# Attention into two dense blocks on one core: fifteen matmuls of the third output moved ahead, a third accumulator bank, and another tile for the convolution's products

## The chip, the core and the metric

The kernel runs on one core of one Trainium2 chip. A core has five instruction streams that run beside one another: TensorE does matmuls and transposes (PE in the profile, with its weight loads as PEld), VectorE is DVE, ScalarE is ACT, GpSimd is POOL, and SyncE (SP) issues the transfers of this kernel. Each engine takes its instructions in a fixed order, and one that waits holds up all behind it on the same engine. The metric is the time of the device in microseconds, the median over runs; less is better.

## The reference, cut to what matters

```python
# q, k, v: (4, 12, 448, 64); weights are 768 x 768, w_tok_*: 448 x 448, 64-bit floats
scores = q @ k.T / sqrt(64), masked above the diagonal
x      = softmax(scores) @ v                     # (4, 448, 768) after joining the heads
gate   = sigmoid(causal convolution of x, 5 taps for each channel)
x      = (gate * (x @ w_val)) @ w_out
theta  = x @ w_theta
y      = w_tok_r @ (x * cos(theta)) + w_tok_i @ (x * sin(theta))   # mixes the 448 positions
u      = x + y
out    = u + relu(u @ w_ch)
```

## The kernel before

The work of a batch falls in two: attention, in six pairs of heads (a pair fills 128 partitions, and makes 128 channels of x), and a dense part of four products with 768 x 768 weights and the token mixing. A product is made in six outputs of 128 channels, numbered n over the whole program: n = 0 to 5 are `w_val`, 6 to 11 `w_out`, and so on. An output takes 18 matmuls (`gemm`, L550): six pieces of the contraction, each with three matmuls, since x and the weights are each split in a high and a low part (`x_hi`, `x_lo`, `w_hl`). The weights come as 64-bit floats. `load_w` fetches half an output (`cv_raw`), `to_f32` makes 32-bit floats of it (DVE L178, ACT, DVE L182, with a bank of PSUM between), and `split_w` the two parts; from n = 3 on POOL does this (L117 high, L120 low).

Batch 0 has nothing to run beside its attention, so a prologue loop of 70 steps does attention of pairs 0 to 6, ten steps each, and the first weights. It also makes outputs 0 and 1 piece by piece, as each pair's x is ready (`gemm_ahead`, L529). After it `dense(b)` runs step by step, with the attention of the next batch woven in at a set rate. A pair's scores are made for pair g while pair g - 1 is transposed and multiplied by v (`attn_iter`). In batch 0 the convolution of pairs 0 to 5 runs on POOL (`attn_X2`, L495 to L502): a gate tile, a tile `tp` for a tap's product, and four adds. `hf` (L590) is gate times output.

Tiles come out of pools by tag: a tag has so many buffers, handed out in turn, and whoever gets a buffer waits until the one before is done with it. `tp` and `hf` share the tag "tmp" with two buffers. `tok_bits` (L191), the raw token weights, and z of the second block have the tag "z" with four. PSUM has eight banks: tag "mm" (accumulators) has two, tag "at" six, for attention's scores, transposes and products and for `to_f32`.

The framework's scheduler orders the instructions of each engine from the program's order, its own model of durations, and explicit constraints (`issue_after`). All transfers are on SP's one queue, which takes them in order. `plain` is a copy in device memory of the converted `w_val` and `w_out`, kept for the later batches.

Of the kernel before, what the change touches and what calls it, by code (L numbers as in the profile page):

```python
# [9 lines left out]
F32 = mybir.dt.float32  # L10
# [19 lines left out]
AHEAD = 2  # L30
# [12 lines left out]
PLAIN = (0, 1)  # L43
# [5 lines left out]
def kernel(  # L49
# [14 lines left out]
    nc = tc.nc  # L64
    B, H, S, D = q.shape
    DM = H * D
    P = 128
    CP = 112
    NC = S // CP
    NP = H // 2  # L70
    NQ = S // D
# [9 lines left out]
    KC = DM // P  # L81
# [3 lines left out]
    KH = KC // 2  # L85
    NW = 4 * KC
# [3 lines left out]
    pool = ctx.enter_context(tc.tile_pool(name="pool", bufs=2))  # L90
    ps = ctx.enter_context(tc.tile_pool(name="ps", bufs=2, space=PSUM))
# [5 lines left out]
    ident = cpool.tile([P, P], F32, name="ident")  # L97
# [13 lines left out]

    def psum(tag):
        at = "mm" if tag == "mm" else "at"
        return ps.tile([P, 512], F32, tag=at, name=f"ps_{tag}", bufs=2 if tag == "mm" else 6)

    def pool_hi(dst, src):
        nc.gpsimd.tensor_scalar(out=dst, in0=src, scalar1=1.0, scalar2=0.0, op0=ALU.mult, op1=ALU.add)  # L117
# [91 lines left out]
    scratch = dram.tile([NW, 2, P, 2 * KH * P], F32, name="scratch")  # L209
    plain = dram.tile([NW, 2, P, KH * P], F32, name="plain")  # L210
    bits = {}
    splits = {}

    def words(t):
        return t.rearrange("p n two -> p (n two)")[:, 0:CV]

    def load_w(n, g):
        if n >= NW:
            return
        e = n % KC  # L220
        t = pool.tile([P, CV, 2], I32, tag="wb", name="cv_raw", bufs=8)
        nc.sync.dma_start(
            out=t.rearrange("p (c n) two -> p c (n two)", c=KH),
            in_=stages[n // KC][g * KH * P : (g + 1) * KH * P, 2 * e * P : 2 * (e + 1) * P].rearrange(
                "(c p) n -> p c n", p=P
            ),
        )
        bits[n, g] = t

    def stage_w(n, g):  # L230
        if n < NW:
            to_f32(words(bits[n, g]), bits[n, g])

    def split_w(n, g):
        if (n, g) not in bits:
            return
        flat = words(bits.pop((n, g))).bitcast(F32)
        t = flat.rearrange("p (c n) -> p c n", n=P)
        kept = n % NW // KC in PLAIN
        if B > 1 and kept and n < NW:  # L240
            nc.sync.dma_start(out=plain[n, g], in_=flat)
        store = B > 1 and (kept and B > 2 if n >= NW else not kept)
        if n < AHEAD:
            hi, lo = (
                pool.tile([P, S], F32R, tag=tag, name="w_ahead", bufs=12)[:, : KH * P].rearrange("p (c n) -> p c n", n=P)
                for tag in ("act_hi", "act_lo")
            )
        else:
            hl = pool.tile([P, 2, KH, P], F32R, tag="wb", name="w_hl", bufs=8)
            hi, lo = hl[:, 0], hl[:, 1]  # L250
        if AHEAD < n < NW:
            pool_hi(hi, t)
        else:
            nc.scalar.copy(hi, t)  # L254
        (dve_lo if n <= AHEAD or n < NW and int(W_DVE[n // KC]) > g else pool_lo)(lo, t, hi)
        if store and n < AHEAD:
            for a, x in enumerate((hi, lo)):
                nc.sync.dma_start(
                    out=scratch[n, g][:, a * KH * P : (a + 1) * KH * P], in_=f32(x.rearrange("p c n -> p (c n)"))
                )  # L260
        elif store:
            nc.sync.dma_start(out=scratch[n % NW, g], in_=f32(hl.rearrange("p a c n -> p (a c n)")))
        splits[n, g] = (hi, lo)
# [22 lines left out]
    x_hl = {}  # L286
# [7 lines left out]
    av_ins = []  # L294
# [118 lines left out]
    def attn_R(g):  # L413
        if not 0 <= g < B * NP:
            return
        rec = pool.tile([P, NQ], F32, tag="rec", name="rec")
        nc.vector.tensor_scalar(out=rec, in0=sums[g], scalar1=1.0e-9, scalar2=None, op0=ALU.add)
        nc.vector.reciprocal(rec, rec)  # L418
        if g < NP:
            wide = pool.tile([P, NQ, D], F32, tag="m2k", name="wide", bufs=2)  # L420
            nc.vector.tensor_tensor(
                out=wide, in0=istack.unsqueeze(1).broadcast_to((P, NQ, D)),
                in1=rec.unsqueeze(2).broadcast_to((P, NQ, D)), op=ALU.mult,
            )
            wides[g] = wide
            return
        pt = psum("tr")
        nc.tensor.transpose(pt[:NQ, :P], rec, ident)
        rect = pool.tile([NQ, 2, D], F32, tag="rect", name="rect", bufs=1)
        nc.vector.tensor_copy(rect, pt[:NQ, :P].rearrange("i (j x) -> i j x", j=2))  # L430
        for j in range(2):
            nc.vector.tensor_copy(rect[0:3, j], pt[0:3, (1 - j) * D : (2 - j) * D])
        rows = dram.tile([2, NQ, D], F32, tag="rows", name="rows", bufs=2)
        nc.sync.dma_start(out=rows[:, 0:5].rearrange("h i x -> i h x"), in_=rect[2:NQ])
        nc.sync.dma_start(out=rows[:, 5:NQ].rearrange("h i x -> i h x"), in_=rect[0:2])
        row_at[g] = rows
# [46 lines left out]
    def attn_X2(g):  # L483
        b, hp = divmod(g, NP)
        x = xf[g % 2]
        gt = pool.tile([P, S], F32, tag="gate", name="gate", bufs=6)
        if CONV_ACT[g]:
            nc.scalar.activation(gt, x[:, 0:S], AF.Copy, scale=cw[:, 0, hp : hp + 1])
            for t in range(1, KW):
                tp = pool.tile([P, S], F32, tag="tmp", name="tp")  # L490
                nc.scalar.activation(tp, x[:, t : t + S], AF.Copy, scale=cw[:, t, hp : hp + 1])
                nc.gpsimd.tensor_tensor(out=gt, in0=gt, in1=tp, op=ALU.add)
        elif CONV_POOL[g]:
            tp = pool.tile([P, S], F32, tag="tmp", name="tp")
            nc.gpsimd.tensor_scalar(  # L495
                out=gt, in0=x[:, 0:S], scalar1=cw[:, 0, hp : hp + 1], scalar2=1.0, op0=ALU.mult, op1=ALU.mult
            )
            for t in range(1, KW):
                nc.gpsimd.tensor_scalar(  # L499
                    out=tp, in0=x[:, t : t + S], scalar1=cw[:, t, hp : hp + 1], scalar2=1.0, op0=ALU.mult, op1=ALU.mult  # L500
                )
                nc.gpsimd.tensor_tensor(out=gt, in0=gt, in1=tp, op=ALU.add)  # L502
        else:
            nc.vector.tensor_scalar(out=gt, in0=x[:, 0:S], scalar1=cw[:, 0, hp : hp + 1], scalar2=None, op0=ALU.mult)
            for t in range(1, KW):
                nc.vector.scalar_tensor_tensor(
                    out=gt, in0=x[:, t : t + S], scalar=cw[:, t, hp : hp + 1], in1=gt, op0=ALU.mult, op1=ALU.add
                )
        gates[b, hp] = gt
        raw_gates.append((b, hp))  # L510
# [6 lines left out]

    wn = [AHEAD]
    ahead = {}

    def gemm_ahead(kc):
        xhi, xlo = x_hl[0, kc]
# [11 lines left out]
                splits.pop((n, 0)), splits.pop((n, 1))  # L534


    def gemm(acts):
        n = wn[0]
        wn[0] += 1
        pt = psum("mm")  # L540
        for g in range(2):
            split_w(n + 1, g)
            stage_w(n + 2, g)
            load_w(n + 3, g)
            fetch_w(n + 3, g)
            whi, wlo = splits.pop((n, g))
            for kc in range(g * KH, (g + 1) * KH):
                xhi, xlo = acts[kc]
                for m, (a, x) in enumerate(((whi, xhi), (whi, xlo), (wlo, xhi))):
                    nc.tensor.matmul(  # L550
                        pt[:, :S], lhsT=a[:, kc % KH, :], rhs=x,
                        start=kc == 0 and m == 0, stop=kc == KC - 1 and m == 2,
                    )
            if g == 0:
                yield
        return pt
# [206 lines left out]
    for n in range(5 * H + 10):  # L763
        next(at, None)
        if n == 5:
            conv_raw = load_conv()
        if n == CONV_AT:
            setup_conv(conv_raw)
        if 1 <= n < 5 * H:
            with tc.issue_after(ttr_ins[-1].ins):  # L770
                for at_n, (m, g) in zip(A_TILES, ((0, 0), (1, 0), (0, 1), (1, 1), (2, 0), (2, 1), (3, 0), (3, 1))):
                    if n == max(W_FROM, at_n - W_AT):
                        load_w(m, g)
                    if n == at_n:
                        stage_w(m, g)
                        if m < AHEAD + 1:
                            split_w(m, g)
        if n >= 25 and n % 10 == 5:
            with tc.issue_after(av_ins[-1].ins):
                gemm_ahead(n // 10 - 2)  # L780
        if n == 5 * H + 9:
            gemm_ahead(KC - 1)
        if n == 5 * H - 3:
            with tc.issue_after(ttr_ins[-1].ins):
                for g in range(2):
                    load_w(AHEAD + 2, g)
# [47 lines left out]
```

## Time and profile before

| what | value |
|---|---|
| median of 3 runs | 699.96 us (698.92 to 702.09) |
| the profiled execution | 701.29 us, span 699.2 us, mean granted clock 0.989 |
| PE busy | 673.4 us, 96% of the span |
| DVE, ACT, POOL busy | 376.4, 358.8 and 302.2 us |

The span is from the first to the last instruction of the profiled execution; 2.09 us of its time lie around it. TensorE is busy nearly throughout, so what another engine does matters where TensorE waits for it. The granted clock is the share of full speed at which TensorE was let run.

### The profile page before, as it was taken

To read this page: it belongs to the slowest core of one execution; us is meant where nothing else is said; L and a number is where in the kernel's file an instruction comes from. 1 tells how busy PE (TensorE), PEld (TensorE's weight loads), DVE (VectorE), ACT (ScalarE), POOL (GpSimd) and SP (SyncE) were. 2 spreads that over 40 slices of the span, in tenths; PEclk is the share of its full clock that TensorE was granted. 3 is DMA by queue.
4 is the path that set the end of the run, shared out by engine and by line. 5 is a ranking of instruction groups with operands and counts; after the bars stand their busy time and mean duration, and the time that the engine had idled before them with its cause. 6 is when DMAs were issued, how large, how long until landed. Compare 5 with 4: busy or idle time off the path is not lost.

```text
span 699.2 us, 12863 instructions
## 1 busy us (share of the span) xinstructions
PE 673.4 (96%) x4595; PEld 582.9 (83%) x4595; DVE 376.4 (54%) x944; ACT 358.8 (51%) x849; POOL 302.2 (43%) x319
## 2 busy tenths in 40 slices
PE   5999799989999999999999999999999999999997
PEld 4777687868888898888898888888888999898996
DVE  4877696668565455345556444544765241126521
ACT  4787486759764545537654234337664221243401
POOL 0599958867485765742663000220601503011100
PEclk9999899999999999999999999999999999999999
DMA  8759478788442999897240776756230578772232
GB/s 212 169 158 228 123 220 267 211 296 249 130 150 71 297 302 301 274 297 193 82 119 13 222 212 213 214 175 184 84 105 14 159 213 222 209 220 69 86 105 66
DMA packets 133030, 124.67 MB, mean 178 GB/s; under 512 B 72905, under 2 KB 110567, under 8 KB 132967
## 3 DMA queue, kind: packets, MB, share of 16 engines
q1 hardware_dynamic: 132967, 123.86, 60.6%
q8 instruction: 36, 0.59, 0.4%
q14 instruction: 27, 0.22, 0.1%
HBM read 94.66 MB, written 29.16 MB: 177 GB/s over the span
## 4 chain that ended last, share of the span: by engine, by line
PE 79%; POOL 7%; DVE 5%; DMA 3%; ACT 3%; issue 2%; SPq 1%; DVEq 0%; POOLq 0%; ACTq 0%
PE ps_mm L550 44%; PE ps_mm L656 15%; PE ps_s L355 5%; PE ps_av L400 5%; PE ps_tr L378 4%; POOL gate L502 2%; PE ps_tr L642 2%; PE ps_tr L328 2%; POOL tp L499 1%; PE ps_tr L683 1%; DMA cv_raw<-in_moe_w_out_dram 1%; DMA cv_raw<-in_moe_w_theta_dram 1%; SPq L303 1%; DVE ps_cv L178 1%; DVE cv_raw L182 1%
## 5 line engine op out<-in xcount | busy, mean ns | idle before, releaser
L550 PE MATMUL ps_mm<-act_hi,w_hl 128*128 128x448 f32 x864 | 268.5, 375 | 2.8 <-POOL w_hl L117 1.1
L550 PEld LDWEIGHTS ps_mm<-act_hi,w_hl 128*128 128x128 f32 x864 | 162.1, 189 | 21.4 <-issue 2.5
L550 PE MATMUL ps_mm<-act_lo,w_hl 128*128 128x448 f32 x432 | 157.1, 364 | 0.0
L132 ACT ACTIVATE prob<-prob,negm 128x448 f32<-128x448 f32 (+6 forms) x168 | 83.9, 501 | 41.8 <-DVE negm L363 41.7
L550 PE MATMUL ps_mm<-x_hi,w_hl 128*128 128x448 f32 x264 | 83.1, 381 | 2.5 <-DVE hf L590 2.5
L550 PEld LDWEIGHTS ps_mm<-act_lo,w_hl 128*128 128x128 f32 x432 | 81.8, 189 | 4.4
L363 DVE CUSTOM_DVE_ANT_0 prob<-ps_s,mask 128x448 f32<-128x448 f32 (+6 forms) x168 | 62.5, 420 | 40.7 <-PE ps_s L355 40.2
L120 POOL TENSOR_TENSOR act_lo<-x2f,act_hi 128x448 fp32r<-128x448 f32 x36 | 41.9, 1164 | 77.7 <-DVE act_hi L562 34.5
L120 POOL TENSOR_TENSOR w_hl<-cv_raw,w_hl 128x384 fp32r<-128x384 f32 x60 | 63.0, 1051 | 19.3 <-ACT w_hl L254 17.6
L120 POOL TENSOR_TENSOR x_lo<-xf,x_hi 128x448 fp32r<-128x448 f32 x22 | 28.1, 1279 | 91.8 <-ACT x_hi L479 91.8
L656 PE MATMUL ps_mm<-wtok_h,zt_h 128*128 128x448 f32 x168 | 63.9, 381 | 0.0
L656 PE MATMUL ps_mm<-wtok_h,zt_l 128*128 128x448 f32 x168 | 62.2, 371 | 0.2 <-DVE zt_l L123 0.2
L656 PE MATMUL ps_mm<-wtok_l,zt_h 128*128 128x448 f32 x168 | 61.5, 366 | 0.0
L355 PE MATMUL ps_s<-kt,qt 64*64 64x256 f32 (+6 forms) x672 | 55.8, 405 | 4.2 <-DVE rec L418 2.1
L502 POOL TENSOR_TENSOR gate<-gate,tp 128x448 f32<-128x448 f32 x48 | 57.0, 1187 | 2.6
L550 PEld LDWEIGHTS ps_mm<-x_hi,w_hl 128*128 128x128 f32 x264 | 50.9, 193 | 7.7 <-DVE hf L590 3.1
L378 PE MATMUL ps_tr<-ident,prob 128*128 128x128 f32 x384 | 54.5, 277 | 0.9 <-DVE cv_raw L182 0.9
L355 PEld LDWEIGHTS ps_s<-kt,qt 64*64 64x64 f32 x672 | 30.1, 136 | 28.7 <-issue 15.9
L633 POOL TENSOR_TENSOR z<-z,x2f 128x448 f32<-128x448 f32 x18 | 21.4, 1191 | 75.1 <-ACT z L628 75.1
L378 PEld LDWEIGHTS ps_tr<-ident,prob 128*128 128x128 f32 x384 | 45.7, 142 | 6.6 <-DVE cv_raw L182 1.4
L400 PEld LDWEIGHTS ps_av<-pt,v 128*64 128x64 f32 x768 | 40.2, 137 | 13.1 <-ACT pt L389 3.2
L400 PE MATMUL ps_av<-pt,v 128*64 128x64 f32 (+3 forms) x768 | 48.0, 277 | 3.0 <-ACT pt L389 3.0
(103 smaller groups left out, 1112.4 us busy)
## 6 DMA issues: line engine op xcount, KB each, us to landing
w_hl<-scratch SPq DMA_DIRECT2D x120, 384.0 KB
scratch<-w_hl SPq DMA_DIRECT2D x48, 384.0 KB
q_raw<-in_q_dram SPq DMA_DIRECT2D x48, 112.0 KB
k_raw<-in_k_dram SPq DMA_DIRECT2D x48, 112.0 KB
out_dram<-o SPq DMA_DIRECT2D x24, 224.0 KB
v<-in_v_dram SPq DMA_DIRECT2D x48, 96.0 KB
cv_raw<-in_moe_w_val_dram SPq DMA_DIRECT2D x12, 384.0 KB
plain<-cv_raw SPq DMA_DIRECT2D x24, 192.0 KB
```

What stands on the lines that cost most here:

```text
L120: nc.gpsimd.tensor_tensor(out=dst, in0=src, in1=f32(hi), op=ALU.subtract)
L132: exps.append(nc.scalar.activation(*args, **kw))
L328: nc.tensor.transpose(pt[:, c * CP : (c + 1) * CP], t[:, c, :, :].rearrange("p h d -> p (h d)"), ident[:CP, :CP])
L355: nc.tensor.matmul(bank[o : o + D, off : off + n], lhsT=qt[j * D : (j + 1) * D, i * D : (i + 1) * D], rhs=kt[j * D : (j + 1) * D, :n], sta ...
L363: ttr = nc.vector.tensor_tensor_reduce(out=probs[i][:, :n], in0=pt, in1=mask[:, S - n : S], scale=-1.0 / math.sqrt(D), scalar=3.0e38, op0= ...
L378: nc.tensor.transpose(pt[:, n * P : (n + 1) * P], probs[i][:, kc * P : (kc + 1) * P], ident)
L400: mm = nc.tensor.matmul(av[g][j * D : (j + 1) * D, lo * D : hi * D], lhsT=tv[:, j, kc, :], rhs=t[:, n0 : n0 + hi - lo, o : o + D], start=( ...
L502: nc.gpsimd.tensor_tensor(out=gt, in0=gt, in1=tp, op=ALU.add)
L550: nc.tensor.matmul(pt[:, :S], lhsT=a[:, kc % KH, :], rhs=x, start=kc == 0 and m == 0, stop=kc == KC - 1 and m == 2,)
L633: (nc.vector if Z_DVE[b] else nc.gpsimd).tensor_tensor(out=t, in0=t, in1=x2f[e], op=ALU.mult)
L642: nc.tensor.transpose(pt[:, (m - m0) * P : (m - m0 + 1) * P], z.rearrange("p a s -> p (a s)")[:, m * P : (m + 1) * P], ident,)
L656: nc.tensor.matmul(pt[:, :S], lhsT=a[:, m, :], rhs=w[:, m, :], start=m == 0 and n == 0, stop=m == NZ - 1 and n == 2,)
```

## The change

Six edits. The accumulators get three banks, and attention and `to_f32` together five. The product tile `tp` of pairs 0 to 5 comes from the tag "z" (four buffers) and no longer from "tmp". `gemm_part` issues 15 of the 18 matmuls of output n = 2, those of pairs 0 to 4, at step 65 of the prologue, when x of pair 5 is not yet made; `gemm` later does the last three. The copy `plain` of a half output is stored when it is converted, one output earlier in the program than before, and behind the latest load of weights. The transpose of pair 6's reciprocals and the last `gemm_ahead` are ordered behind the matmuls that stand ahead of them.

```diff
@@ def psum(tag)
-        return ps.tile([P, 512], F32, tag=at, name=f"ps_{tag}", bufs=2 if tag == "mm" else 6)
+        return ps.tile([P, 512], F32, tag=at, name=f"ps_{tag}", bufs=3 if tag == "mm" else 5)
@@ def load_w(n, g)
-        nc.sync.dma_start(
+        loads.append(nc.sync.dma_start(
...
+    def keep_w(n, g):
+        if B > 1 and n < NW and n // KC in PLAIN:
+            with tc.issue_after(loads[-1].ins):
+                nc.sync.dma_start(out=plain[n, g], in_=words(bits[n, g]).bitcast(F32))
@@ def split_w(n, g)
-        if B > 1 and kept and n < NW:
-            nc.sync.dma_start(out=plain[n, g], in_=flat)
@@ def attn_R(g)
-        nc.tensor.transpose(pt[:NQ, :P], rec, ident)
+        with ExitStack() as st:
+            if g == NP:
+                st.enter_context(tc.issue_after(av_ins[-1].ins))
+            nc.tensor.transpose(pt[:NQ, :P], rec, ident)
@@ def attn_X2(g)
-            tp = pool.tile([P, S], F32, tag="tmp", name="tp")
+            if g < NP:
+                tp = pool.tile([P, 2, S], F32, tag="z", name="tp", bufs=4)[:, 0, :]
+            else:
+                tp = pool.tile([P, S], F32, tag="tmp", name="tp")
@@ after def gemm_ahead(kc)
+    def gemm_part():
+        n = AHEAD
+        part[n] = psum("mm")
+        for kc in range(KC - 1):
+            xhi, xlo = x_hl[0, kc]
+            whi, wlo = splits[n, kc // KH]
+            for m, (a, x) in enumerate(((whi, xhi), (whi, xlo), (wlo, xhi))):
+                mm = nc.tensor.matmul(
+                    part[n][:, :S], lhsT=a[:, kc % KH, :], rhs=x,
+                    start=kc == 0 and m == 0, stop=False, skip_group_check=True,
+                )
+        av_ins.append(mm)
@@ def gemm(acts)
-        pt = psum("mm")
+        first = KC - 1 if n in part else 0
+        pt = part.pop(n) if n in part else psum("mm")
...
+            keep_w(n + 2, g)
...
-            for kc in range(g * KH, (g + 1) * KH):
+            for kc in range(max(first, g * KH), (g + 1) * KH):
@@ the prologue loop
+                        keep_w(m, g)
...
+        if n == 5 * H + 5:
+            with tc.issue_after(av_ins[-1].ins):
+                gemm_part()
         if n == 5 * H + 9:
-            gemm_ahead(KC - 1)
+            with tc.issue_after(av_ins[-1].ins):
+                gemm_ahead(KC - 1)
```

What this does to the order on the engines is seen in three places. First TensorE at the end of the prologue. Before, the share of pair 4 in outputs 0 and 1 (L529) is followed by pair 6's transposed reciprocals (L428), pair 5's share, and output 2 as a whole (L550):

```order
L529 MATMUL ps_mm<-x_lo,w_ahead 128x448
L529 MATMUL ps_mm<-x_hi,w_ahead 128x448
L428 MATMUL ps_tr<-ident,rec 7x128
L529 MATMUL ps_mm<-x_hi,w_ahead 128x448 x2
L529 MATMUL ps_mm<-x_lo,w_ahead 128x448
L529 MATMUL ps_mm<-x_hi,w_ahead 128x448
L529 MATMUL ps_mm<-x_lo,w_ahead 128x448
L529 MATMUL ps_mm<-x_hi,w_ahead 128x448
L550 MATMUL ps_mm<-x_hi,w_hl 128x448
L550 MATMUL ps_mm<-x_lo,w_hl 128x448
L550 MATMUL ps_mm<-x_hi,w_hl 128x448 x2
```

In the changed kernel fifteen matmuls of output 2 (L555) stand ahead of the transpose (now L435); three of output 2 (now L576) are mixed in with pair 5's share of outputs 0 and 1 (now L540):

```order
L555 MATMUL ps_mm<-x_hi,w_hl 128x448
L435 MATMUL ps_tr<-ident,rec 7x128
L540 MATMUL ps_mm<-x_hi,w_ahead 128x448 x2
L576 MATMUL ps_mm<-x_hi,w_hl 128x448
L540 MATMUL ps_mm<-x_lo,w_ahead 128x448
L540 MATMUL ps_mm<-x_hi,w_ahead 128x448
L540 MATMUL ps_mm<-x_lo,w_ahead 128x448
L540 MATMUL ps_mm<-x_hi,w_ahead 128x448
L576 MATMUL ps_mm<-x_lo,w_hl 128x448
L576 MATMUL ps_mm<-x_hi,w_hl 128x448
L382 MATMUL ps_tr<-ident,prob_77 128x128 x4
```

Behind them stand the same eight transposes of probabilities, output 3 and the scores of pair 7 in both kernels; only the fifteen have moved.

Second the queue of SP, from the loads of the fifth pair on. Before, the four parts of the first two chunks of the token weights (L193, the chunks c = 0 and 1, each w_tok_r and w_tok_i) go out together, ahead of the loads of q, k and v of the pairs that follow:

```order
L193 DMA tok_bits<-in_moe_w_tok_r_dram 112x896
L193 DMA tok_bits<-in_moe_w_tok_i_dram 112x896
L241 DMA plain<-cv_raw 128x384
L222 DMA cv_raw<-in_moe_w_val_dram 128x3x256
L193 DMA tok_bits<-in_moe_w_tok_r_dram 112x896
L193 DMA tok_bits<-in_moe_w_tok_i_dram 112x896
L303 DMA q_raw<-in_q_dram 112x4x64 x2
L303 DMA k_raw<-in_k_dram 112x4x64 x2
```

In the changed kernel they stand behind those loads, the fourth of them (w_tok_i of chunk 1) behind pair 6's reciprocals, and ahead of chunk 2, two copies and the first loads of `w_out` (now L223):

```order
L319 DMA v_79<-in_v_dram 64x2x64
L193 DMA tok_bits<-in_moe_w_tok_r_dram 112x896
L193 DMA tok_bits<-in_moe_w_tok_i_dram 112x896
L193 DMA tok_bits<-in_moe_w_tok_r_dram 112x896
L441 DMA rows<-rect 5x2x64
L442 DMA rows<-rect 2x2x64
L470 DMA rb<-rows 64x448 x2
L193 DMA tok_bits<-in_moe_w_tok_i_dram 112x896
L193 DMA tok_bits<-in_moe_w_tok_r_dram 112x896
L193 DMA tok_bits<-in_moe_w_tok_i_dram 112x896
L238 DMA plain<-cv_raw 128x384 x2
L223 DMA cv_raw<-in_moe_w_out_dram 128x3x256 x2
```

The tag "z" is why: its first six tiles are now the `tp` of pairs 0 to 5, so the parts of chunks 0 and 1 get the buffers of the `tp` of pairs 2, 3, 4 and 5 in this order, and the transfer into each waits for the last add of that convolution.

Third VectorE, where the numbers behind the names tell buffers apart. Before, from output 2's hf on; `tok_bits_1196` and `1202` are chunk 2, `cv_raw_1146` is the first half of output 5, and prob6 is the first of pair 7's softmax:

```order
L590 SCALAR_TENSOR_TENSOR hf_1189<-gate_657,ps_mm_1137 128x448
L182 SCALAR_TENSOR_TENSOR cv_raw_961<-cv_raw_961,ps_cv_1174 128x384
L178 TENSOR_SCALAR ps_cv_1198<-tok_bits_1196 112x448
L178 TENSOR_SCALAR ps_cv_1204<-tok_bits_1202 112x448
L178 TENSOR_SCALAR ps_cv_1228<-cv_raw_1146 128x384
L123 TENSOR_TENSOR act_lo_1192<-hf_1189,act_hi_1191 128x448
L590 SCALAR_TENSOR_TENSOR hf_1274<-gate_802,ps_mm_1223 128x448
L182 SCALAR_TENSOR_TENSOR tok_raw_1195<-tok_bits_1196,ps_cv_1198 112x448
L363 ISA prob6_77,negm_1039<-ps_s_1208,mask_67 128x448
```

In the changed kernel, from output 3's hf on; `tok_bits_1204` is the fourth part, w_tok_i of chunk 1, and `cv_raw_1162` the first half of output 5:

```order
L616 SCALAR_TENSOR_TENSOR hf_1276<-gate_802,ps_mm_1225 128x448
L123 TENSOR_TENSOR act_lo_1194<-hf_1191,act_hi_1193 128x448
L178 TENSOR_SCALAR ps_cv_1206<-tok_bits_1204 112x448
L182 SCALAR_TENSOR_TENSOR tok_raw_1197<-tok_bits_1198,ps_cv_1200 112x448
L178 TENSOR_SCALAR ps_cv_1229<-cv_raw_1162 128x384
L367 ISA prob6_77,negm_1041<-ps_s_1210,mask_67 128x448
L367 ISA negm_1041 128x1
L367 ISA prob4_75,negm_1041<-ps_s_1213,mask_67 128x320
L367 ISA negm_1041 128x1
L367 ISA prob1_72,negm_1041<-ps_s_1213,mask_67 128x128
L123 TENSOR_TENSOR act_lo_1279<-hf_1276,act_hi_1278 128x448
L182 SCALAR_TENSOR_TENSOR cv_raw_1162<-cv_raw_1162,ps_cv_1229 128x384
```

A token load is still read between hf of output 3 and pair 7's softmax, and output 5's conversion stands behind it, as before; but the load is now the fourth part and not a part of chunk 2.

## Rows read from the trace of the kernel before

**Rows 1.** The page, its first section: busy us of each engine, share, instructions.
```profile
PE 673.4 (96%) x4595; PEld 582.9 (83%) x4595; DVE 376.4 (54%) x944; ACT 358.8 (51%) x849; POOL 302.2 (43%) x319
```
**Rows 2.** Windows: length, busy us of PE, PEld, DVE, ACT, POOL, granted clock, DMA share, GB/s.
```profile
50.00:85.00 35.00, 30.34 (x265) 24.73 (x264) 22.71 (x68) 21.66 (x64) 33.18 (x38) 0.90 0.72 177
80.00:100.00 20.00, 20.00 (x124) 16.31 (x125) 19.00 (x46) 14.28 (x36) 13.20 (x16) 0.91 0.66 200
...
112.00:150.00 38.00, 36.49 (x247) 30.09 (x244) 24.55 (x57) 24.17 (x56) 31.99 (x37) 1.00 0.77 238
150.00:160.00 10.00, 6.98 (x59) 5.59 (x59) 8.56 (x27) 8.55 (x19) 5.22 (x7) 0.83 0.95 321
...
170.00:600.00 430.00, 430.00 (x2934) 376.30 (x2933) 219.41 (x536) 209.71 (x489) 175.12 (x172) 1.00 0.60 177
```
**Rows 3.** Timeline of PE: start, us, work; in brackets the idle time before, and its releaser.
```profile
72.55 0.27 PE L428 MATMUL ps_tr<-ident,rec 128*7 128x128 f32 x1 [0.38 <-DVE rec L418]
73.75 0.68 PE L529 MATMUL ps_mm<-x_hi,w_ahead 128*128 128x448 f32 x2 [0.93 <-ACT x_hi L479]
...
78.08 0.74 PE L550 MATMUL ps_mm<-x_hi,w_hl 128*128 128x448 f32 x1 [2.53 <-DVE hf L590]
...
84.23 0.37 PE L550 MATMUL ps_mm<-x_hi,w_hl 128*128 128x448 f32 x1
...
85.23 0.45 PE L550 MATMUL ps_mm<-x_hi,w_hl 128*128 128x448 f32 x1
...
89.00 0.99 PE L355 MATMUL ps_s<-kt,qt 64*64 64x448 f32 x12
89.92 0.47 PE L550 MATMUL ps_mm<-x_hi,w_hl 128*128 128x448 f32 x1
...
93.89 0.36 PE L550 MATMUL ps_mm<-x_hi,w_hl 128*128 128x448 f32 x1
...
95.52 0.47 PE L550 MATMUL ps_mm<-x_hi,w_hl 128*128 128x448 f32 x1
...
103.19 0.45 PE L550 MATMUL ps_mm<-act_hi,w_hl 128*128 128x448 f32 x1
```
**Rows 4.** Windows of 1 us, PE alone: length, busy, granted clock, DMA share, GB/s.
```profile
77.00:78.00 1.00, 0.00 (x0) 0.50 0.03 13
```
**Rows 5.** Timeline of POOL.
```profile
86.46 0.51 POOL L117 TENSOR_SCALAR w_hl<-cv_raw 128x384 fp32r<-128x384 f32 x1
87.05 1.02 POOL L120 TENSOR_TENSOR w_hl<-cv_raw,w_hl 128x384 fp32r<-128x384 f32 x1
...
89.02 1.00 POOL L120 TENSOR_TENSOR w_hl<-cv_raw,w_hl 128x384 fp32r<-128x384 f32 x1
...
102.66 1.15 POOL L120 TENSOR_TENSOR x_lo<-xf,x_hi 128x448 fp32r<-128x448 f32 x1
```
**Rows 6.** Timeline of SP's queue.
```profile
58.40 0.50 SPq L193 DMA_DIRECT2D tok_bits<-in_moe_w_tok_i_dram  x1
```
**Rows 7.** Timeline of DVE.
```profile
77.41 0.62 DVE L590 SCALAR_TENSOR_TENSOR hf<-gate,ps_mm 128x448 f32<-128x448 f32 x1 [2.41 <-POOL gate L502]
...
85.75 1.15 DVE L178 TENSOR_SCALAR ps_cv<-tok_bits 112x448 int32<-112x448 uint32 x2
...
90.25 0.62 DVE L363 CUSTOM_DVE_ANT_0 prob<-ps_s,mask 128x448 f32<-128x448 f32 x1
...
91.33 0.55 DVE L182 SCALAR_TENSOR_TENSOR cv_raw<-cv_raw,ps_cv 128x384 int32<-128x384 int32 x1
...
98.75 0.57 DVE L182 SCALAR_TENSOR_TENSOR cv_raw<-cv_raw,ps_cv 128x384 int32<-128x384 int32 x1
```
**Rows 8.** The chain that ended last: start, us, what.
```profile
102.27 3.69 DMA cv_raw<-in_moe_w_out_dram
...
147.20 5.82 DMA cv_raw<-in_moe_w_theta_dram
```
**Rows 9.** Timeline of PE in the prologue.
```profile
34.79 1.19 PE L378 MATMUL ps_tr<-ident,prob 128*128 128x128 f32 x8 [0.41 <-DVE cv_raw L182]
```

More of the change, by code (lines that the diff above doesn't have):

```diff
@@ L211 @@
     bits = {}
+    loads = []
     splits = {}
@@ L226, in load_w @@
             ),
-        )
+        ))
         bits[n, g] = t
@@ L519 @@
     ahead = {}
+    part = {}
     def gemm_ahead(kc):
@@ L551, in gemm @@
                         pt[:, :S], lhsT=a[:, kc % KH, :], rhs=x,
-                        start=kc == 0 and m == 0, stop=kc == KC - 1 and m == 2,
+                        start=kc == 0 and m == 0, stop=kc == KC - 1 and m == 2, skip_group_check=first > 0,
                     )
```

## Prediction

> **What bounds the kernel now.** I read the page first: TensorE is busy for 673.4 us of the span [rows 1]. The windows then show that its idle time is not spread. From 170 to 600 us it is busy for 430.00 of 430 us; the waits lie ahead of that, 1.51 us of idle time in 112 to 150 and 3.02 in 150 to 160, where the mean clock is also only 0.83 [rows 2]. From 80 to 100 us the reader is to see something else: DVE is busy for 19.00 of 20 us beside a full TensorE, so whatever holds DVE there delays everything it makes [rows 2]. From 50 to 85, POOL has 33.18 of 35 us: convolutions and weight splits [rows 2].
>
> The timeline of PE shows the spot of the change. PE waits 0.38 us for pair 6's reciprocals, 0.93 for pair 5's x, and 2.53 for hf of output 0, which holds the accumulator bank that output 2 needs [rows 3]. That hf itself is released by the last add of pair 4's convolution: its buffer of "tmp" was `tp` [rows 7]. So 3.84 us of idle time, and a second cost: the clock falls to 0.50 (1.2 of 2.4 GHz) by 77 us, when PE has done little since 72 [rows 4]. Output 2 pays for it: 17 matmuls from start to start in 84.23 - 78.08 = 6.15 us, 0.362 each, where output 3 takes 89.00 - 85.23 = 3.77 us for 18, or 0.209 [rows 3].
>
> **The change part by part.** *The fifteen matmuls, the third bank, the two ordered transposes.* Fifteen of output 2's matmuls fill the holes: at most 3.84 us of waits and 15 x (0.362 - 0.209) = 2.3 us of slow pace, 6.1 us. That is what they could give; I follow PE on. It is free at 72.55 - 0.38 = 72.17, the fifteen end at 72.17 + 15 x 0.209 = 75.3, the transpose (0.27) and nine matmuls at 77.5 (x of pair 5 was there at 73.75), eight transposes at 78.3 (0.79, from the end of output 2 at 84.23 + 0.21 to 85.23), output 3 at 82.0, twelve score matmuls (89.92 - 89.00) at 83.0 [rows 3]. Before, it stood there at 89.92: nearly 7 us are won. But next is output 4, whose weights POOL makes behind the whole convolution of pair 5: high part 86.46 + 0.51 = 86.97, low part at 88.07, second half until 90.02 [rows 5]. POOL's order there is the same in both kernels, and POOL had 1.82 us of idle time in 35 [rows 2], so the weights hardly come earlier. PE would wait from 83.0 to 87 or later, as long as the hole that was filled. Where it waits that long the clock would fall again, as it did around 77 us: output 4 at 0.362 takes 18 x 0.362 = 6.5 us and ends near 94.1, where it ended before (93.89 + 0.2) [rows 3]. At full pace it would end 2.9 us earlier (89.92 - 86.97). Bounds -2.9 and 0; I take **0**, because the hole (4.6 us with the next item) is no shorter than the one whose clock I saw.
>
> *Five banks for attention.* A bank wait of this kind is in the trace: the transposes of pair 2 wait 0.41 us for a conversion's L182 [rows 9]. With one bank less the same use waits for one holder later; I count it for three pairs of the prologue, where PE is early enough for it. Below 0 (POOL works from a backlog), at most 3 x 0.41 = 1.2 us on POOL's chain; I take half, 0.6, so that the weights come at 87.6. Later PE shows no wait for a bank at all (430.00 of 430 [rows 2]); there I cost it at nothing, and the rival below prices it.
>
> *tp in the tag of the token loads.* `hf` of outputs 0 and 1 no longer waits for a convolution; that is in the gain above. But the token parts now wait for convolutions. Before, the first four were sent off by 58.40 + 0.50 [rows 6]; now the fourth waits for pair 5's last add, at 86.46 + 0.6 = 87.1 [rows 5]. Nothing is hidden here, since SP takes its transfers in order: behind it stand chunk 2, two copies and two loads of `w_out`, and behind the DVE instruction that reads it (L178) stand output 5's conversion and pair 7's softmax. The price is its landing. The chain has two loads of about this size, 3.69 and 5.82 us [rows 8]. I take 3.69, the nearer in time and neighbours, so it is there at 90.8. DVE then does L178 (half of 1.15), an L182 (0.55) and an L178 of weights (0.5, near the L182), and pair 7's softmax starts at 92.4 in place of 90.25, +2.2 [rows 7]. Output 5's L182 stands three softmax pieces, an act_lo and an L182 behind that; at about 0.46 each by start-to-start distances of at most 0.55, 2.3 us, it starts at 94.7, not 91.33: +3.4 [rows 7]. Output 5 on PE hardly feels it (before, PE came to it at 95.52, 4.2 us behind the conversion [rows 3, 7]): 94.7 + 0.55 + 0.51 + 1.02 = 96.8 against a third matmul at 95.9. Output 6 does. From one L182 to the other there were 98.75 - 91.33 = 7.4 us; in the new order two token L178 (1.15), an L178 of weights, xf and rec come in between and two softmax pieces and an act_lo go out, which is 1.2 more by such durations: 103.3, +4.6 [rows 7]. On POOL pair 6's x_lo (1.15) now stands between the high and low part: 103.3 + 0.57 + 0.51 + 1.15 + 1.02 = 106.5 [rows 5]. PE needed that part for its third matmul at 103.19 + 0.42 = 103.6 [rows 3]. So PE is **2.9** us late there. With a landing of 5.82 it is 5.0; if a transfer landed within the 1.5 us that would leave the softmax where it was, 0.
>
> The Trainium skill ("DMA: Bandwidth & Descriptors", section "Anatomy of one DMA — SWDGE (gpsimd) path") gives 2.0 us and the bytes over 436 GB/s for one transfer, as a fit for that other path; for 112 x 896 words of 4 bytes that is an estimate of 2.9 us, and the sum would be 0.8 lower. The two rows of this trace, 3.69 and 5.82 us for nearly as many bytes, are both longer, and they decide.
>
> *The copies* (`plain`) are the same in number and size, issued an output earlier and behind a load. Two of them stand between the token parts and the loads of `w_out`; a token load takes 0.50 us to issue [rows 6], and two copies twice as much at most, on loads that SP sends behind a longer wait. I take 0, at most +0.5.
>
> *What is given back later.* From 112 to 160 PE idles for 1.51 + 3.02 = 4.5 us and loses 0.17 x 10 = 1.7 us to the clock [rows 2]. A TensorE that is late waits less there, as far as those it waits for are not late too. They are mostly transfers, POOL and DVE on the same chain [rows 8], so I take a third of 6.2: **-2.1** (bounds 0 and -6.2).
>
> **Sum:** 0 + 2.9 - 2.1 = +0.8 us on the profiled execution's 701.29 us. That execution is 1.33 above the median shown, 699.96, so the time to expect beside that median is 700.8 us. About half a percent (3.5 us) is what a measurement of this kernel can tell from no change.
>
> **Rivals.** *Faster.* The fill is kept: output 4 starts with its high part at 86.97 at full clock, 2.9 us early, and a third of the later waits goes as well: -5.0, 695.0 us. For it speaks that output 5 has 4.2 us of slack towards DVE and that POOL, not DVE, set output 4; against it that the token part would have to land within 1.5 us, and DVE has 1 us of idle time in 20 [rows 2]. Chance 0.20. The Trainium skill ("Perfetto Trace Analysis", section "Matmuls") would have groups of matmuls rotate through different banks, so that emptying one overlaps with filling the next; that is this rival. The trace agrees on the first bank (2.53 us behind hf), not on what follows.
>
> *Slower.* The fourth token part lands as late as the 5.82 of the theta weights, output 6 is 5.0 us late, and nothing is given back, because the transfers of `w_out` behind it in SP's queue are as late: 705.0 us. It decides when lateness less recovery is above 3.5, so from a landing of about 5 us with a recovery below 0.8. For it: the theta row, and transfers that are shared with q, k, v and copies; against: the idle time ahead of 160. Chance 0.22.
>
> *Five banks cost in every pair.* If each of the 18 pairs of batches 1 to 3 paid one wait of 0.41 us, 7.4 us more: 708.2. PE's 430.00 of 430 speaks against it [rows 2]. Chance 0.05.
>
> That the fifteen do not run where they stand I exclude: their x and weights are used just before or wait for nothing in the trace, and the bank is new.
>
> **How the numbers follow.** Forecast, within half a percent, 0.53: 698 to 703. Range 695.0 to 706.0: it leaves out the bank rival and the ends of the two others. Faster by over 0.5%: 0.20; same 0.53; slower 0.22 + 0.05 = 0.27.
>
> **What would show it.** The holes at 72 and 75 to 78 are gone, and a hole of 4 to 5 us stands ahead of output 4, from about 83, with the clock near 0.50 behind it; POOL's first L117 behind the convolution is still near 86.5 to 87.1. The fourth token part is issued at 87, its L178 on DVE waits for a transfer, pair 7's softmax starts near 92.4, output 6's conversion near 103.3. From 170 on PE is full. I am wrong if that hole is below 2 us or the clock stays up, if the fourth part is issued well ahead of 86, if DVE passes it without a wait, or if PE waits for banks beyond 170.

## Result and profile after

The changed kernel takes 705.41 us in the median of 5 runs (704.37 to 706.29), beside 700.13 for the kernel before, measured with it. The ratio is 1.007, with a 95% interval of 1.0052 to 1.0089. So it is slower by 5.3 us: inside the range that was given, but in the case to which I gave 0.27, not in the one I forecast. The profiled execution took 705.41 us, its span is 703.3.

What the prediction walked through is there, most of it within a microsecond. First the windows (length; busy us of PE, PEld, DVE, ACT, POOL; granted clock, DMA share, GB/s), to hold against [rows 2]:

```profile
50.00:85.00 35.00, 33.20 (x299) 28.04 (x299) 24.91 (x74) 24.92 (x71) 33.18 (x38) 1.00 0.66 168
80.00:100.00 20.00, 15.84 (x82) 11.46 (x83) 15.57 (x38) 11.78 (x29) 12.85 (x15) 0.83 0.67 213
...
112.00:150.00 38.00, 37.34 (x253) 30.64 (x252) 24.59 (x59) 25.71 (x61) 32.75 (x38) 1.00 0.81 238
150.00:160.00 10.00, 9.14 (x78) 7.42 (x76) 8.14 (x19) 8.90 (x19) 6.33 (x8) 1.00 1.01 344
160.00:170.00 10.00, 7.74 (x44) 6.11 (x45) 8.98 (x24) 9.92 (x22) 6.65 (x8) 1.00 0.93 254
170.00:600.00 430.00, 430.00 (x2913) 373.22 (x2912) 219.84 (x539) 210.42 (x490) 175.28 (x171) 1.00 0.59 176
```

TensorE's hole has moved: from 50 to 85 us it is busier by 2.9 us at full clock, and from 80 to 100 it idles for 4.16 us and has a mean clock of 0.83. The waits of 112 to 160 shrank from 4.5 to 1.5 us, with 2.26 us behind them up to 170 (0.43 before). From 170 on the row says 430.00 of 430 as before; that row misled me, as will be seen. Now the timeline of PE, against [rows 3]:

```profile
76.20 0.37 PE L555 MATMUL ps_mm<-x_hi,w_hl 128*128 128x448 f32 x1
76.40 0.27 PE L435 MATMUL ps_tr<-ident,rec 128*7 128x128 f32 x1
...
82.61 0.37 PE L576 MATMUL ps_mm<-x_hi,w_hl 128*128 128x448 f32 x1
84.69 1.44 PE L359 MATMUL ps_s<-kt,qt 64*64 64x448 f32 x12 [1.71 <-DVE tok_raw L182]
88.40 0.74 PE L576 MATMUL ps_mm<-x_hi,w_hl 128*128 128x448 f32 x1 [2.27 <-POOL w_hl L117]
...
106.72 0.67 PE L576 MATMUL ps_mm<-act_hi,w_hl 128*128 128x448 f32 x2 [1.27 <-POOL w_hl L120]
```

The waits at 72, 73 and 78 us are gone; in their place are 1.71 us ahead of pair 7's scores and 2.27 ahead of output 4, whose weights release it. Behind that the clock is at half. POOL, SP and DVE show why, against [rows 5 to 7]; first POOL:

```profile
86.49 1.37 POOL L512 TENSOR_TENSOR gate<-gate,tp 128x448 f32<-128x448 f32 x1
87.84 0.51 POOL L117 TENSOR_SCALAR w_hl<-cv_raw 128x384 fp32r<-128x384 f32 x1
...
104.09 0.51 POOL L117 TENSOR_SCALAR w_hl<-cv_raw 128x384 fp32r<-128x384 f32 x1 [3.60 <-DVE cv_raw L182]
104.56 1.14 POOL L120 TENSOR_TENSOR x_lo<-xf,x_hi 128x448 fp32r<-128x448 f32 x1
105.66 1.00 POOL L120 TENSOR_TENSOR w_hl<-cv_raw,w_hl 128x384 fp32r<-128x384 f32 x1
```

SP's queue, the fourth token part:

```profile
87.89 0.35 SPq L193 DMA_DIRECT2D tok_bits<-in_moe_w_tok_i_dram  x1
```

And DVE:

```profile
91.30 0.63 DVE L178 TENSOR_SCALAR ps_cv<-tok_bits 112x448 int32<-112x448 uint32 x1 [4.43 <-DMA tok_bits<-in_moe_w_tok_i_dram]
...
92.83 0.61 DVE L367 CUSTOM_DVE_ANT_0 prob<-ps_s,mask 128x448 f32<-128x448 f32 x1
...
95.06 0.55 DVE L182 SCALAR_TENSOR_TENSOR cv_raw<-cv_raw,ps_cv 128x384 int32<-128x384 int32 x1
...
103.45 1.01 DVE L182 SCALAR_TENSOR_TENSOR cv_raw<-cv_raw,ps_cv 128x384 int32<-128x384 int32 x2
```

The token part is issued at 87.89, as the convolution ends, and DVE idles for 4.43 us at the instruction that reads it. Pair 7's softmax, output 5's and output 6's conversions follow at 92.83, 95.06 and 103.45. The prediction had 87.1, 92.4, 94.7 and 103.3, and output 6's third matmul 2.9 us late; it is at 106.72, and was at 103.68 before, so 3.0 late:

```profile
103.68 0.56 PE L550 MATMUL ps_mm<-act_hi,w_hl 128*128 128x448 f32 x2
```

The weights of output 4 came later than I had them: GpSimd's first L117 behind the convolution is at 87.84, 1.4 us later than before, where I had allowed for 0.6.

So the stretch that I costed came out as costed, and yet the kernel is 5.3 us slower and not 0.8. To find the rest I follow one instruction of each pair, the multiplication that makes its x (DVE, xf), in both timelines. Its lateness against the same instruction of the kernel before, from the starts there, for this kernel and three of the experiments below:

| pair (its start before, us) | changed | banks alone | six banks, tp in z | both undone |
|---|---|---|---|---|
| 5 (72.47) | +1.1 | +3.1 | +0.1 | +0.7 |
| 6 (100.96) | +2.0 | -1.1 | +1.4 | +1.5 |
| 9 (189.01) | +1.3 | +3.1 | +3.9 | 0.0 |
| 16 (382.20) | +3.1 | +4.9 | +3.9 | 0.0 |
| 23 (570.73) | +4.9 | +7.9 | +4.1 | -0.1 |

In the first column only 1.3 us of lateness are left at 189 us. It grows by 3.6 us after that, in the stretch where TensorE's row shows no idle time. A lateness at 189 us is otherwise kept to the end, as the third and fourth column show. The rows of pairs 9 and 23, first in the kernel before (L474), then in the changed one (L481):

```profile
189.01 0.62 DVE L474 TENSOR_TENSOR xf<-ps_av,rb 128x448 f32<-128x448 f32 x1
570.73 0.63 DVE L474 TENSOR_TENSOR xf<-ps_av,rb 128x448 f32<-128x448 f32 x1 [4.39 <-DMA rb<-rows]
...
190.33 0.62 DVE L481 TENSOR_TENSOR xf<-ps_av,rb 128x448 f32<-128x448 f32 x1
575.66 0.62 DVE L481 TENSOR_TENSOR xf<-ps_av,rb 128x448 f32<-128x448 f32 x1 [4.57 <-DMA rb<-rows]
```

### The profile page after: what moved, and what is told of

It is laid out like the page before. It is cut to its first block, busy times and chain, and to the rows that moved or that the text cites. A ratio compares the mean times of both kernels' runs of the same rounds, so it can differ in the third digit from the quotient of the medians.

```text
span 703.3 us, 12835 instructions
## 1 busy us (share of the span) xinstructions
PE 679.1 (97%) x4595; PEld 582.5 (83%) x4595; DVE 376.3 (53%) x944; ACT 359.7 (51%) x849; POOL 302.8 (43%) x319
## 4 chain that ended last, share of the span: by engine, by line
PE 78%; ACT 5%; POOL 5%; DVE 5%; DMA 4%; issue 2%; SPq 1%; DVEq 0%; ACTq 0%; POOLq 0%
PE ps_mm L576 43%; PE ps_mm L682 15%; PE ps_s L359 5%; PE ps_tr L382 5%; PE ps_av L404 4%; PE ps_tr L668 2%; POOL gate L512 2%; DMA cv_raw<-in_moe_w_theta_dram 2%; PE ps_tr L332 2%; PE ps_tr L709 1%; ACT prob L132 1%; POOL tp L509 1%; DVE ps_cv L178 1%; SPq L307 1%; DVE cv_raw L182 1%
## 5 line engine op out<-in xcount | busy, mean ns | idle before, releaser
L576 PE MATMUL ps_mm<-act_hi,w_hl 128*128 128x448 f32 x864 | 265.3, 374 | 2.2 <-POOL w_hl L120 1.7
L576 PEld LDWEIGHTS ps_mm<-act_hi,w_hl 128*128 128x128 f32 x864 | 160.8, 188 | 21.3 <-issue 3.1
L576 PE MATMUL ps_mm<-act_lo,w_hl 128*128 128x448 f32 x432 | 157.1, 364 | 0.0
L576 PEld LDWEIGHTS ps_mm<-act_lo,w_hl 128*128 128x128 f32 x432 | 81.3, 188 | 4.7 <-issue 0.2
L576 PE MATMUL ps_mm<-x_hi,w_hl 128*128 128x448 f32 x254 | 79.3, 379 | 2.3 <-POOL w_hl L117 2.3
L359 PE MATMUL ps_s<-kt,qt 64*64 64x320 f32 (+6 forms) x672 | 62.8, 412 | 5.5 <-DVE rec L422 2.8
L359 PEld LDWEIGHTS ps_s<-kt,qt 64*64 64x64 f32 x672 | 32.0, 139 | 33.9 <-issue 17.7
L576 PEld LDWEIGHTS ps_mm<-x_hi,w_hl 128*128 128x128 f32 x254 | 48.3, 191 | 7.5 <-POOL w_hl L117 2.5
L393 ACT COPY pt<-ps_tr 128x512 f32<-128x512 f32 x66 | 37.2, 579 | 21.3 <-PE ps_tr L382 21.2
```

What stands on the lines that cost most here:

```text
L359: nc.tensor.matmul(bank[o : o + D, off : off + n], lhsT=qt[j * D : (j + 1) * D, i * D : (i + 1) * D], rhs=kt[j * D : (j + 1) * D, :n], sta ...
L393: nc.scalar.copy(dst, src)
L576: nc.tensor.matmul(pt[:, :S], lhsT=a[:, kc % KH, :], rhs=x, start=kc == 0 and m == 0, stop=kc == KC - 1 and m == 2, skip_group_check=first ...
```

## Experiments

Two theories. **P:** the loss is in the prologue, from the token part that waits for pair 5's convolution. **B:** five attention banks change the order that the scheduler makes, and the cost lies beyond 170 us. In the order the scores of a pair (4 and 8 matmuls into two banks, then 16 more; the profile counts two for each that the program issues) stand in more pieces, each of which is a visit of TensorE to the scores; most pieces take about 0.9 us, with 4 matmuls as with 16. Not all do, and the kernel before shows what sets it. A piece's time runs from its start to that of the next instruction:

```profile
174.14 0.97 PE L355 MATMUL ps_s<-kt,qt 64*64 64x448 f32 x4
175.04 0.47 PE L656 MATMUL ps_mm<-wtok_h,zt_h 128*128 128x448 f32 x1
...
175.65 0.76 PE L355 MATMUL ps_s<-kt,qt 64*64 64x320 f32 x4
176.33 0.47 PE L656 MATMUL ps_mm<-wtok_h,zt_l 128*128 128x448 f32 x1
...
178.56 0.44 PE L355 MATMUL ps_s<-kt,qt 64*64 64x128 f32 x4
178.92 0.47 PE L656 MATMUL ps_mm<-wtok_h,zt_h 128*128 128x448 f32 x1
```

Four matmuls take 0.90 us with 448 columns, 0.68 with 320 and 0.36 with 128. The kernel (`side`) places the four of 448 on other 64 by 64 parts of the array than the eight of 320 and 128 columns, which together have 448 as well. Either half takes 0.90 alone, and the whole twelve 0.92: the halves run beside one another. A cut between the two banks makes them run one after the other, which is why it costs nearly a whole piece, while one that splits off only the four of 128 costs 0.35 (0.90 and 0.37, not 0.92). So "whatever its size" in the expectations below does not hold; for the cuts between the banks the 0.9 does.

**Banks alone.** The kernel before with one line of the change:

```diff
-bufs=2 if tag == "mm" else 6)
+bufs=3 if tag == "mm" else 5)
```

> The kernel before with three accumulator banks and five for attention, and nothing else of the change. Theory P (prologue): the loss comes from the fourth token part, which waits for the convolution of pair 5 and holds up VectorE; then this kernel is within 1.5 us of the kernel before, 699 to 701.5. Theory B (banks): with five banks the order that the scheduler makes cuts the scores of a pair into more visits of TensorE, each of which takes some 0.9 us whatever its size, and the cost lies beyond 170 us; then it is 2 to 4 us slower, 702 to 704, with two or three visits more beyond 170 us than the 33 of before.

706.57 us, ratio 1.0092 (1.0072 to 1.0111): slower by itself than the whole change, and beyond both ranges. In its timeline of PE the first scores of a pair stand in two pieces:

```profile
372.33 0.97 PE L355 MATMUL ps_s<-kt,qt 64*64 64x448 f32 x4
373.23 0.47 PE L656 MATMUL ps_mm<-wtok_h,zt_h 128*128 128x448 f32 x1
...
375.56 0.37 PE L656 MATMUL ps_mm<-wtok_h,zt_l 128*128 128x448 f32 x1
375.86 0.97 PE L355 MATMUL ps_s<-kt,qt 64*64 64x320 f32 x8
376.76 0.47 PE L656 MATMUL ps_mm<-wtok_h,zt_h 128*128 128x448 f32 x1
```

The first piece holds PE from 372.33 to 373.23 and the second from 375.86 to 376.76, 0.90 us each. In the kernel before, the twelve stand together, for 0.92 us:

```profile
368.54 0.99 PE L355 MATMUL ps_s<-kt,qt 64*64 64x448 f32 x12
369.46 0.47 PE L656 MATMUL ps_mm<-wtok_h,zt_h 128*128 128x448 f32 x1
```

Nothing waits there: a piece is busy time. P falls as the whole account, B holds for 4.8 us by their place (+3.1 to +7.9 in the table), of which the pieces make 3.6 (32.07 us in all beyond 170, not 28.49); the +3.1 at 189 us comes on top, and neither theory had it.

**tp in another tile.** The changed kernel with

```diff
-                tp = pool.tile([P, 2, S], F32, tag="z", name="tp", bufs=4)[:, 0, :]
+                tp = pool.tile([P, S], F32, tag="x2f", name="tp", bufs=6)
```

> The changed kernel with tp of pairs 0 to 5 in the buffers of x2f (free until the second product) in place of z, so that no token part waits for a convolution; banks as changed. Theory P: nearly all of the 5.3 us come back, 700 to 701.5, and output 6 starts on TensorE about 3 us sooner. Theory B: only what lay ahead of 170 us comes back, 0.5 to 1.5 us, 704 to 705, unless the new order happens to cut the scores less often.

704.75 us, ratio 1.0071 (1.005 to 1.0092). No token part waits for a convolution any more, and 0.7 us come back by the medians, nothing by the ratios (1.007 for the changed kernel): as B said, against P.

**The early matmuls in an attention bank.** The changed kernel with

```diff
-bufs=3 if tag == "mm" else 5)
+bufs=2 if tag == "mm" else 6)
...
-        part[n] = psum("mm")
+        part[n] = psum("tr")
```

> The changed kernel with two accumulator banks and six for attention again; the fifteen early matmuls write into one of the attention banks, which is given back after output 2. tp stays in z. Theory P: the token part is as late as before, 704 to 706. Theory B: the scores are cut as seldom as before (about 33 visits beyond 170 us) and some 3.5 us come back, 701 to 702.5.

704.49 us, ratio 1.0058 (1.0035 to 1.008). The lateness beyond 189 us stays flat, as B said, but the sum does not come back: the kernel is 3.9 us late at 189, and its time lies in P's range, not in B's. Here P has its share:

```profile
90.33 0.63 DVE L178 TENSOR_SCALAR ps_cv<-tok_bits 112x448 int32<-112x448 uint32 x1 [4.51 <-DMA tok_bits<-in_moe_w_tok_i_dram]
```

**Both.** These two edits together.

> Both edits: tp in the buffers of x2f, and the fifteen early matmuls in an attention bank, with two and six banks. Theory P: as the kernel with tp moved alone, 700 to 701.5. Theory B: 699 to 700.5. In both, TensorE still waits ahead of output 4, since its weights come behind the convolution of pair 5 on GpSimd.

700.83 us, ratio 1.0001 (0.9984 to 1.0018): the whole loss is gone, as both theories had it. Beside the kernel with six banks and tp in z, only tp's tile differs, and 3.7 us; beside the one with tp moved and five banks, only the banks (and with them that of the early matmuls), and 3.9 us. Each is worth that where the other is not there. Together they cost 4.6 us and not 7.6, since with five banks the order of the prologue is another one; how the two share what is lost there I leave open. The piece of scores is whole again:

```profile
368.53 0.99 PE L359 MATMUL ps_s<-kt,qt 64*64 64x448 f32 x12
```

**Five banks without a third accumulator.** The kernel before with `bufs=2 if tag == "mm" else 5`.

> The kernel before with two accumulator banks and five for attention: one of the eight banks is left unused. It tells whether the sixth attention bank or the third accumulator matters. If the loss is that of the attention bank, as I now hold, it is slower by about as much as three and five banks were, 703 to 707; its order has the scores of four more pairs in three visits in place of two. Were it the third accumulator that let the order slip, it would be within 1.5 us of before, 699 to 701.5.

710.36 us, ratio 1.0136 (1.0109 to 1.0163; one execution of 1680 us, which no other kernel had, is left out): slower than the range I gave. So it is the sixth attention bank that counts; with the third accumulator in use the loss was less (1.0092), in that one order. Its first trace was of that odd execution, so I took another:

> The kernel before with two accumulator banks and five for attention once more, for its trace. By its order it has 35 visits to the scores beyond 170 us, so the cuts give about 3 us there; the other 6 to 7 us of its 9.6 must then be lateness at 190 us, as the kernel with three and five banks had 3.1 there. If the lateness at 190 us is below 4 us, the cuts are not what five banks cost.

One run, 709.9 us. The lateness of xf is +5.4 at pair 9 and +8.9 at pair 23: 3.6 beyond 189 us, where the cuts are, and 5.4 ahead of that, where I had expected 6 to 7. So more than half of the cost of this kernel is not the cuts; what makes it I did not follow up.

**The cuts by themselves.** The kernel before, banks untouched, with the first scores of some pairs written as two steps:

```diff
-        attn_S(g, 0)
+        if g in SPLIT:
+            attn_S(g, 0, slice(0, 1))
+        else:
+            attn_S(g, 0)
...
         yield
+        if g in SPLIT:
+            attn_S(g, 0, slice(1, 2))
         attn_PT(h, 2)
```

> The kernel before, its banks and all else as they are, with the first scores of ten of the pairs from 11 on written as two parts a step apart; the order that comes out has four visits more beyond 200 us (4 and 8 score matmuls in place of 12), and is the same ahead of that. It measures the visit by itself. If a visit of TensorE to the scores takes some 0.9 us whatever its size, 4 x 0.9 = 3.6 us slower, 703 to 704.5. If the five banks cost by their waits and not by the cuts, no more than 1 us slower, 700 to 701.5.

704.54 us, ratio 1.0055 (1.0036 to 1.0075), for four pieces more. Two of them in its timeline of PE:

```profile
344.12 0.97 PE L356 MATMUL ps_s<-kt,qt 64*64 64x448 f32 x4
...
347.03 0.97 PE L356 MATMUL ps_s<-kt,qt 64*64 64x320 f32 x8
```

The lateness of xf goes from -0.2 at pair 9 to +4.5 at pair 23, 1.2 us a cut where I had 0.9. That is the price of a cut measured alone, with no bank fewer. The pieces make 0.9 of it (32.01 us in all, not 28.49). Around a piece the starts are also further apart: 0.30 us between the matmul ahead (343.82) and the piece, and between the two behind it (345.02 and 345.32), where matmuls of this kind otherwise start 0.20 apart; that is 0.2 more a cut. The changed kernel has two pieces more than before beyond 170 us (35, not 33), but four of before's were short (4 matmuls of 128 or 320 columns, 0.36 to 0.68 us); all of its own took 0.89 or more. Summed to the next instruction, pieces take 32.03 us there, not 28.49: 3.5 us more, of the 3.6 by which the lateness grew.

**The copies.** Both edits, with `plain` stored where the kernel before stores it.

> The kernel with both edits, but the copies (plain) stored where the kernel before stores them. If the earlier copies, which stand ahead of loads in SyncE's queue, cost something, 0.5 to 2 us faster than the kernel with both edits; if I was right to cost them at nothing, within 0.7 us of it, 699.5 to 701.5.

700.05 us, ratio 0.999 (0.9971 to 1.001): no difference that can be told.

**What holds the fill up.** If output 4's weights stood behind less on GpSimd, could TensorE keep its lead? Both edits, and the convolution of pair 5 on VectorE (`CONV_POOL[5] = 0`):

> tp in the buffers of x2f, early matmuls in an attention bank, and the convolution of pair 5 on VectorE in place of GpSimd, so that output 4's weights no longer stand behind it. My theory of the fill: TensorE's wait of 3.0 us ahead of output 4 goes, and the clock stays up there. If TensorE's lead lasts, 694 to 697. If what comes behind binds anyway (the transfer of a theta weight at 147 us and the conversions after it stood at the same time in the kernel with both edits as before), 699 to 700.5.

699.63 us, ratio 0.9982 (0.9965 to 0.9998). And that convolution's move alone in the kernel before:

> The kernel before with the convolution of pair 5 on VectorE alone, as a control for the kernel that has it together with the early matmuls. If GpSimd's load sets the stretch from 86 to 150 us, 2 to 4 us faster than before, 696 to 698; if not, 699 to 701.

701.62 us, ratio 1.0008 (0.9989 to 1.0026). Neither gains what I had hoped: in the first the wait ahead of output 4 shrinks from 3.03 us to 0.17, but 0.90 us ahead of output 5 and 1.32 and 1.06 ahead of output 6 come, for GpSimd's weights again, with VectorE ahead of it busy for 18.45 us of the 20 from 70 to 90. The wait ahead of output 4 with both edits, and then with the convolution moved too:

```profile
88.23 0.74 PE L576 MATMUL ps_mm<-x_hi,w_hl 128*128 128x448 f32 x1 [3.03 <-POOL w_hl L117]
```
```profile
86.51 0.47 PE L576 MATMUL ps_mm<-x_hi,w_hl 128*128 128x448 f32 x1 [0.17 <-POOL w_hl L117]
```

Next, its products on ScalarE (`CONV_ACT[5] = 1`, tp in the buffers of x2f) with the adds left on GpSimd:

> tp in the buffers of x2f, early matmuls in an attention bank, and pair 5's convolution with its products on ScalarE and its four adds on GpSimd. GpSimd has some 3 us less ahead of output 4's weights and VectorE nothing more. If the lead of the fill can be kept by freeing GpSimd without loading VectorE, 2 to 4 us faster than before, 696 to 698. If the stretch beyond 100 us binds anyway, as with the convolution on VectorE, 699 to 701.

698.7 us, ratio 0.9977 (0.9962 to 0.9992). A small gain. TensorE now does this between the early matmuls and output 4:

```profile
74.86 0.37 PE L555 MATMUL ps_tr<-x_hi,w_hl 128*128 128x448 f32 x1
...
81.28 0.37 PE L576 MATMUL ps_mm<-x_hi,w_hl 128*128 128x448 f32 x1
83.43 2.56 PE L359 MATMUL ps_s<-kt,qt 64*64 64x448 f32 x12 [1.79 <-DVE hf L616]
85.92 0.74 PE L576 MATMUL ps_mm<-x_hi,w_hl 128*128 128x448 f32 x1
```

It waits for an hf of VectorE, and the clock falls to half while the scores run. That hf reads `ps_tr`, the attention bank in which the early matmuls stand, and the scores start as it ends:

```profile
82.77 0.61 DVE L616 SCALAR_TENSOR_TENSOR hf<-gate,ps_tr 128x448 f32<-128x448 f32 x1
```

So the fill, as placed here, holds up the scores itself: it takes one of the six attention banks until output 2 is done. The last kernel takes the fill away and keeps the rest of that one:

```diff
-        if n == 5 * H + 5:
+        if False:
```

> The kernel with tp in the buffers of x2f and pair 5's convolution on ScalarE and GpSimd, but without the fifteen early matmuls (two and six banks; output 2 is made as a whole in an accumulator). It tells what the fill itself is worth once GpSimd is free. If the fill is what gained there, this one is 1 us or more slower than that kernel, 700 to 701.5. If freeing GpSimd and the accumulator's hf was enough, it is as fast, 698 to 699.5.

695.86 us, ratio 0.9934 (0.9911 to 0.9957): faster than the kernel before, than every kernel here and than either range. I had expected the fill to be what gained. Its timeline of PE:

```profile
72.40 0.27 PE L435 MATMUL ps_tr<-ident,rec 128*7 128x128 f32 x1 [0.37 <-DVE rec L422]
73.59 0.67 PE L540 MATMUL ps_mm<-x_hi,w_ahead 128*128 128x448 f32 x2 [0.93 <-ACT x_hi L486]
...
83.14 0.36 PE L576 MATMUL ps_mm<-x_hi,w_hl 128*128 128x448 f32 x1
83.43 0.99 PE L359 MATMUL ps_s<-kt,qt 64*64 64x448 f32 x12
84.34 0.47 PE L576 MATMUL ps_mm<-x_hi,w_hl 128*128 128x448 f32 x1
```

The scores of pair 7 start at 83.43 in both, in the one behind a wait for VectorE, here with no wait. Without the early matmuls their 3.0 us of work (15 x 0.2) fill the place ahead of it, and the two holes of 0.37 and 0.93 us stay; the hole of 1.79 us is gone, and from 50 to 112 us the clock stays at 1.00. The piece of scores takes 0.91 us and not 2.5. Output 4 starts 1.6 us sooner, and the lateness of xf at pair 9 is -5.2 us, not -2.9. GpSimd's weights of output 4 come earlier as well (its L117 at 82.61, not 85.07 behind a wait of 2.22 us for a conversion on VectorE). No run has the fill in a bank that nobody else needs, so what it would be worth there stays open. Nor does one have tp's move or the products on ScalarE by themselves, without the fill: the 0.66% are those of both, with the earlier copies and the ordered transposes, which that kernel keeps.

## Why the prediction was right and wrong

The range held, and by luck: its upper end came from the rival in which the token part lands after 5.82 us and nothing is given back, and neither came to pass. The part landed in 3.4 us, and the time came near that end by a cost that was in no term. The forecast, no change, was wrong, and one step of it failed.

*The fill* was right at worth nothing, since the hole comes back ahead of output 4 with the clock down. Its last place was where I put it, the weights of POOL. The scores of pair 7 waited 1.71 us as well, for VectorE's L182, which I had not seen. That instruction reads `ps_cv`, one of the five banks, so by the code this is a wait for a bank, longer than the 0.41 I had counted. Output 4's weights came behind it anyway; in the kernel with the fill and the products on ScalarE a wait at this place, for another bank, was 1.79 us.

*The token part* was right in each of its times (above), and its price without the bank change is 3.7 us by the pair of kernels that differ in nothing else.

*Given back later* was right in sign: 3.0 us late at output 6, 1.3 at 189 us, so 1.7 where I had 2.1.

*Five banks for attention* is the step that failed, the term "there I cost it at nothing". I looked for waits for a bank, found 430.00 of 430, and took that as proof. But the scheduler turned the missing bank into another order, in which the scores are cut, and that price is busy time. 3.6 us of lateness beyond 189 us is the measured term in place of 0. The rival that priced it had the right place and the wrong mechanism (a wait in each of 18 pairs, 7.4 us), and I gave it 0.05. The cut was there to be seen before the run: the order of the changed kernel shows 4 and 8 score matmuls where there were 12, and in the timeline of the kernel before a piece of 8 takes 0.91 us (to the matmul at 95.52), where one of 12 takes 0.92 in [rows 3] (89.00 to 89.92):

```profile
94.61 0.98 PE L355 MATMUL ps_s<-kt,qt 64*64 64x384 f32 x8
```

*The clock* was right: 0.50 behind the hole.

*The copies* at nothing: right.

The sum by measured terms: 1.3 us at pair 9 and 3.6 from there to pair 23 are 4.9; after the last pair 0.8 of it comes back, and the span is 4.1 us longer. The medians differ by 5.3; the profiled execution of the kernel before was itself slower than its median by 1.2 us, which is the difference.

## What to carry to other kernels

A buffer taken from one tag is a change to the order of everything that uses the tag. Compare the order over the whole program, not only near the edit, and price a group of small instructions that is cut in two by what each piece takes alone: where its parts ran beside one another, the cut costs a whole part.

Before work is moved into a hole, look for what releases the instruction behind the hole. Here the early matmuls only moved the hole, and in the bank they took they made the scores wait; moving the tile that made the accumulator wait, together with taking pair 5's products off GpSimd, gave 0.66% without them.

A tile that shares a tag with a load makes the load wait for it, and in a queue that keeps its order all loads behind that.

## What the runs showed of the hardware

A visit of TensorE to the 64 by 64 matmuls of the scores held it for 0.90 us with 4 matmuls of 448 columns, 0.90 with 8, 0.92 with 12 and 0.93 with 16, but for 0.68 with 4 of 320 and 0.36 with 4 of 128. The first four cost nearly as much as all of a group, since the others ran beside them; a cut between them made the pairs behind it about 1.2 us late.

The Trainium skill ("TensorEngine Tiling (Array Packing)", section "Key Properties") states that a change of the tiling mode drains TensorE. That would make each cut cost two such changes more. The price of a cut here, 1.2 us, does not speak against it, and neither do the 0.2 us by which the starts around a piece stand further apart, but no run here separates the drain from the matmuls themselves.

Two short holes of 0.37 and 0.93 us left the granted clock at 1.00 in the last kernel, where a wait of 1.71 us, the scores and the start of a wait of 2.27 had it at 0.50 by 87 us:

```profile
87.00:88.00 1.00, 0.00 (x0) 0.00 (x0) 0.00 (x0) 0.00 (x0) 1.00 (x2) 0.50 0.00 0
88.00:89.00 1.00, 0.60 (x2) 0.50 (x2) 0.00 (x0) 0.00 (x0) 0.92 (x2) 0.50 0.25 36
```

These are windows of the changed kernel: PE does nothing in the first, and half the clock holds on into output 4.
